# Half-wide diagonal blocks in the last batch and in the first two chunks, with reordered loads

## The chip, the cores and the metric

The kernel runs on one core of one Trainium2 chip. The metric is the device time of one execution in microseconds (us); smaller is better. Five engines work side by side, each on its own list of instructions in a fixed order, and they wait for one another through semaphores: TensorE (PE, matmul), whose weight loads the profile lists apart as PEld; VectorE (DVE); ScalarE (ACT); GpSimd (POOL), which does almost nothing here; and SyncE (SP), which issues the DMAs.

## The reference

Eight independent attentions without softmax, multiplied by `u`, feed a soft mixture of experts over all 19968 tokens.

```python
# u, v: (8, 2496, 256)   z: (8, 2496, 64)
scores = (1 / S) * np.matmul(z, z.transpose(0, 2, 1))
attn = np.maximum(scores, 0.0) ** 2
x = (u * np.matmul(attn, v)).reshape(B * S, D)
logits = x @ phi                                  # 32 slots, 4 for each of 8 experts
# softmax over all tokens -> slot_input = d.T @ x -> two-layer expert on each slot
# softmax over slots -> output = c @ slot_out
```

The scores of one batch form a symmetric matrix, because both factors are the same `z`. The kernel uses that: of a pair of blocks on the two sides of the diagonal it computes one, and gets the other by transposing it.

## The kernel before, in words

**Tiling.** The tokens of one batch are 20 tiles of 128 keys. Four tiles make a block `p` (0 to 4), and each batch has five query chunks `ch` of 512 columns (the fifth has 448; in the last batch the 448-wide chunk 4 stands first, and chunk 3 comes as two of 256). The unit of work is a *half*: two of a block's four key tiles (`w` is 0 or 1) against one chunk. A batch has 50 halves, the last one 60, the program 410; `h` counts them through, `at` is the place in the chunk. The tuple `MEETS` (`FIRST_MEETS` for batch 0) is the table that sets which blocks a chunk meets in which order. A plain number stands for both halves of a block, a pair such as `(2, 0)` for one half alone.

**One half.** `prepare(k)` (L311) makes the attention weights of half `k`: `scores(k)` on PE into the PSUM tile `sc`, Relu and Square on ACT into `r`, then a split of `r` into a rounded part `ph` and a remainder `pl`, so that three fast products (`ph` with both parts of `v`, `pl` with the high part) replace one slow one. `sums_halves` or `sums_whole` (L417, L451) multiply these with the split `v` into the accumulator `acc`. The first is used when a half ahead needs scores on PE; it runs as two phases with matmuls on 64 rows, paired on the two halves of the array, and `prepare` of the half two or three ahead goes between the phases. The second uses all 128 rows. For `k` under `RAW_SCORES` the scores come from unsplit `z` with slow fp32 matmuls, because the split `z` is not ready yet; otherwise from the split `z` in three products.

**Three kinds of half.** If the block on the other side of the diagonal has been done, the half is *turned*: its `r` is fetched from DRAM and no scores are computed. If its block will be wanted by a later chunk, DVE transposes `r` into a tile `y`, and `store` writes it out. A block on the diagonal is its own mirror: where it stands in the table as two pairs, the first half *lends* (DVE transposes 256 of its columns into `yd`, `lend` writes them to DRAM with four DMAs), and the second *borrows* (`borrow` reads them into `rd` with one DMA, its scores are only 256 columns wide, and ACT and DVE split the borrowed and the own part apart). Before the change that is done in batches 1 to 6 and in chunks 2 to 4 of batch 0.

**What sets the order.** Nothing is scheduled by a planner: every engine runs its instructions in the order in which the program writes them. The loop over `h` issues transfers (`transfers`, L767), the sums of half `h`, and the preparation of a half further on. Lists hold work that is run at fixed places in the next `prepare`: `turning` before the split of `r`, `behind` at its end (L368).

**Loads of the next batch.** In the loop from L757, `z_at` and `v_at` (L760) tell at which half, counted from the start of the batch before, the split of each block of `z` and of each of the ten tiles of `v` is due. The DMA is issued two halves earlier. The split (an ACT copy to the high part, a DVE subtraction for the low part) is appended to `behind` at that half and so stands at the end of the `prepare` that runs in it. Tile `i` of `v` holds the two key tiles of block `i // 2`, `w = i % 2`. The 16 buffers of `z` and `v` go round, 15 to a batch, so a tile takes over the buffer that the tile before it in the list had in the batch before.

**Opening of the program.** `opening` lists the loads of batch 0, `open_loads` issues them as the four raw buffers come free, and `keep_busy(n)` issues `n` pairs of filler matmuls on zeros into a tile `idle` that nobody reads.

Of the kernel before, what the change touches and what calls it, by code (L numbers as in the profile page):

```python
# [17 lines left out]
B, S, D, DQK = 8, 2496, 256, 64  # L18
N = B * S
E_, SE, FF = 8, 4, 1024  # L20
NS = E_ * SE
# [3 lines left out]
NQ = 5  # L25
# [4 lines left out]
NP = KT // 4  # L30
# [7 lines left out]
MEETS = (  # L38
# [3 lines left out]
)  # L42
FIRST_MEETS = ((0, 1, 2, 3, 4), (1, 0, 2, 4, 3)) + MEETS[0][2:]

FIRST_Z = {8: 1, 9: 2, 10: 4, 11: 3}

RAW_SCORES = 12

PAD = 224

# [1 line left out]
def f32(ap):  # L52
    return ap.bitcast(F32)
# [14 lines left out]
def attn_soft_moe_kernel(ctx, tc, uT, v, zz, phi, ww, outT):  # L68
    nc = tc.nc

    pe, act, dve, sp = (InOrder(tc, x) for x in (nc.tensor, nc.scalar, nc.vector, nc.sync))
# [48 lines left out]
    def load_v(b, i):  # L120
        raw = raws.tile([P, 2, D], F32, tag="raw", name=f"vr_{b}_{i}", bufs=NRAW)
        sp.dma_start(raw, v[b, :, 2 * i : 2 * i + 2, :])

        def split():
            t = vt_[b, i]
            (dve.tensor_copy if (b, i) == (0, 1) else act.copy)(t[:, :, 0], raw)
            dve.tensor_sub(t[:, :, 1], raw, f32(t[:, :, 0]))

        return split

    opening = []
    for p in range(NP):
        two = [(load_v, 2 * p), (load_v, 2 * p + 1)]
        opening += [(load_z, p)] + (two[::-1] if p == NQ - 1 else two)
    z_splits, v_splits = {}, []

    def open_loads(m):

        while opening and (len(v_splits) < m or opening[0][0] is load_z):
            f, j = opening.pop(0)
            if f is load_z:
                z_splits[j] = f(0, j)
            else:
                v_splits.append(f(0, j))


    ident = cpool.tile([P, P], F32, name="ident")
# [39 lines left out]
    def chunks(b):  # L189
        if b < B - 1:  # L190
            return [(j, 0, min(QC, S - j * QC), b * S + j * QC) for j in range(NQ)]
        t0 = b * S
        out = [(NQ - 1, 0, ROT, t0)]
        out += [(j, 0, QC, t0 + ROT + j * QC) for j in range(NQ - 2)]
        j = NQ - 2
        return out + [(j, o, QC // 2, t0 + ROT + j * QC + o) for o in (0, QC // 2)]
# [19 lines left out]
    halves = []  # L216
    for b in range(B):
        for ch, meets in zip(chunks(b), MEETS[b == B - 1] if b else FIRST_MEETS, strict=True):
            order = []
# [8 lines left out]

    pend, arriving, scratch, staged = {}, {}, {}, {}
    flag = cpool.tile([1, 1], F32, name="flag")
# [2 lines left out]
    middle, behind, stores, turning = [], [], [], []  # L236

    def run(todo):
        now, todo[:] = todo[:], []
        for f in now:  # L240
            f()
# [17 lines left out]
    def scores(k):  # L259
# [21 lines left out]

        if k < RAW_SCORES:
            for h, rows in enumerate(HALF):
# [16 lines left out]
    def high_low(k):  # L300

        if halves[k].ch[2] >= PAD + PAD:
            return [wa.tile([P, 2, QC], F32R, tag=t, name=f"{t}_{k}", bufs=4) for t in ("ph", "pl")]
        i, j = divmod(k % 4, 2)
        if i not in quarters:
            quarters[i] = [
                wa.tile([P, 2, 2, QC // 2], F32R, tag=t, name=f"{t}_{k}", bufs=4) for t in ("ph", "pl")
            ]
        return [t[:, j] for t in quarters[i]]

    def prepare(k):  # L311

        x = halves[k]
        n = x.ch[2]

        parts = [slice(0, 1), slice(1, 2)] if k < 2 else [slice(0, 2)]
        if x.turned:
            whole = arriving.pop(k)
            run(middle)
        else:  # L320
            r = wa.tile([P, 2, QC], F32, tag="r", name=f"r_{k}", bufs=4)
            ps, m = scores(k)
            for h in parts:
                act.activation(r[:, h, :m], ps[:, h, :m], AF.Relu, scale=1.0 / S)
                run(middle)
                act.activation(r[:, h, :m], r[:, h, :m], AF.Square)
            whole = r[:, :, :m].rearrange("p h (a r) -> p h a r", r=P // 2 if x.borrows else P)
        hi, lo = high_low(k)
        m = QC if x.padded else n
        hc, lc = (t[:, :, :m].rearrange("p h (a r) -> p h a r", r=P) for t in (hi, lo))  # L330
        cast = act.copy if x.turned or (x.turns and x.at % 3) else dve.tensor_copy
        run(turning)
        pieces = [(whole, slice(0, P), cast)]
        if x.borrows:
            lent = arriving.pop(k)
            pieces = [(lent, slice(0, P // 2), act.copy), (whole, slice(P // 2, P), dve.tensor_copy)]
        for h in parts:
            for src, cols, cast in pieces:
                cast(hc[:, h, :, cols], src[:, h])
                dve.tensor_sub(lc[:, h, :, cols], src[:, h], f32(hc[:, h, :, cols]))  # L340
        pend[k] = hi, lo
        if x.turns:
            key = x.b, x.ch[0], x.p
            first = key not in staged
            if first:
                staged[key] = turns_sb.tile([P, 16, 4, NS], F32, tag="y", name=f"y_{k}")
            y = staged[key]

            def turn():
                dve.transpose(  # L350
                    y.rearrange("p m i q -> p i m q")[:, 2 * x.w : 2 * x.w + 2],
                    r.rearrange("p h (m q) -> p h m q", q=NS),
                )
                if not first:
                    stores.append((k + (k < 2 * NP), lambda: store(key)))

            if k < 2 * NP:
                turning.append(turn)
            else:
                turn()  # L360
        if x.lends:
            y = turns_sb.tile([P, 4, 2, 2, NS], F32, tag="yd", name=f"yd_{k}", bufs=1)
            dve.transpose(
                y.rearrange("p a j i q -> p i a j q"),
                r.rearrange("p h (a i q) -> p h a i q", i=4, q=NS)[:, :, :, 2:4],
            )
            stores.append((k - 1, lambda: lend(x, y)))
        run(behind)  # L368

    def lend(x, y):  # L370

        key = x.b, x.p, x.p
        t = scratch[key] = dram.tile([P, 4, P], F32, tag="lent", name="lent_%d_%d" % key[:2], bufs=4)
        for a in range(4):
            sp.dma_start(
                t.rearrange("(b q) a r -> q b a r", b=4)[:, :, a],
                y[32 * a : 32 * a + 32].rearrange("q b j i k -> q b (j i k)"),
            )
# [8 lines left out]
    def store(key):  # L387

        y = staged.pop(key)
        t = scratch[key] = dram.tile([P, 4, QC], F32, tag="turned", name="turned_%d_%d_%d" % key)  # L390
        for a in range(4):
            sp.dma_start(
                t.rearrange("(b q) a r -> q b a r", b=4)[:, :, a],
                y[32 * a : 32 * a + 32].rearrange("q (b j) i k -> q b (j i k)", b=4),
            )
# [361 lines left out]
    for b in range(1, B):  # L757
        base, order = (b - 1) * 2 * NP * NQ, BLOCKS[b == B - 1]
        z_at = [29, 31, 33, 39, 41]
        v_at = [47, 42, 43, 44, 45, 46, 48, 49, 50, 51]  # L760
        for j, at in zip(order, z_at):
            splits.setdefault(base + at, []).append((load_z, b, j))
        for i, at in enumerate(v_at):
            splits.setdefault(base + at, []).append((load_v, b, i))
# [24 lines left out]
    def split_first_v():  # L789
        if v_splits:  # L790
            v_splits.pop(0)()
            open_loads(NRAW)
# [20 lines left out]
    def keep_busy(n):  # L813
        for _ in range(n):
            for h, rows in enumerate(HALF):
                pe.matmul(idle[:, h], zero[rows, 0:P], zero[rows], start=True, stop=True)

    take_blocks(0)
    open_loads(NRAW)
    keep_busy(7)  # L820
    split_first_v()
    split_first_v()
    prepare(0)
    prepare(1)
    keep_busy(5)
    constants()
    acc = None
    for h, x in enumerate(halves):
# [11 lines left out]
        if ahead and not halves[ahead[0]].turned:  # L840
            turn = sums_halves(h, acc, 0, None)
            prepare(ahead.pop(0))
            sums_halves(h, acc, 1, turn)
        else:
            if ahead and not x.ends:
                prepare(ahead.pop(0))
            elif not ahead:
                run(middle)
                run(behind)
                between_last(3 - last)  # L850
            sums_whole(h, acc)
# [12 lines left out]
    q = NQG - 1  # L864
    x = xg_.pop(q)
# [274 lines left out]
```

## Time and profile before

| what | value |
|---|---|
| median of 3 runs | 1359.9 us (1359.09 to 1360.61) |
| the profiled execution | 1361.58 us, its span 1359.8 us |
| PE busy | 1336.1 us, 98% of the span |
| DVE busy | 1084.2 us, 80% |
| ACT busy | 908.7 us, 67% |
| mean granted TensorE clock | 0.984 |

All attention work stands under one line of the code, since a helper records every instruction; rows are told apart by the names of the tiles: `sc`, `r`, `ph`, `pl`, `acc`, `y`, `yd`, `rd`, `v`, `vr` (raw `v`), `z`, `zr`, `cw` (which holds the raw `z` of batch 0), `xg` (a finished chunk), `lg` (logits and slot sums). In a timeline row the first number is the start in us from the start of the span, the second how long the merged instructions took, `xN` their count, and the brackets tell how long the engine was idle before and what ended that. A matmul on 64 rows comes in pairs that run together. The fillers and all other matmuls are told by the same two columns.

### The profile page before, as it was taken

How to read it: one execution, taken by the hardware profiler on the slowest of the kernel's cores; microseconds unless marked ns; L12 is line 12 of the kernel's file. 1: busy time of each engine (PE TensorE's matmuls, PEld its weight loads, DVE VectorE, ACT ScalarE, POOL GpSimd, SP SyncE). 2: the span in 40 equal slices, each digit the busy share in tenths (PEclk: the TensorE clock that was granted, in tenths of full speed). 3: DMA queues.
4: the chain of work that ended last, by engine and by line, in shares of the span. 5: the costliest groups of instructions: out<-in, count | busy, mean ns of one | idle time of the engine just before them, and what ended most of it. 6: DMA issues, size and time to landing. Idle time of an engine off the chain costs nothing.

```text
span 1359.8 us, 27351 instructions
## 1 busy us (share of the span) xinstructions
PE 1336.1 (98%) x10929; PEld 1062.3 (78%) x10929; DVE 1084.2 (80%) x1444; ACT 908.7 (67%) x1093; POOL 3.7 (0%) x22
## 2 busy tenths in 40 slices
PE   9999999999999999999999999999999999999985
PEld 6777887778777888778877788778877788778952
DVE  7878897779868898688987889797986889876563
ACT  8866686668755687566856678566875668654453
POOL 0000000000000000000000000000000000000000
PEclk9999999999999999999999999999999999999985
DMA  6568677675758667686776666777585776769969
GB/s 204 158 186 253 206 191 223 196 242 162 221 172 286 211 161 211 183 255 204 191 225 190 230 202 165 226 240 256 142 237 164 243 234 176 219 167 303 361 271 378
DMA packets 132511, 297.28 MB, mean 219 GB/s; under 512 B 17440, under 2 KB 36896, under 8 KB 120608
## 3 DMA queue, kind: packets, MB, share of 16 engines
q1 hardware_dynamic: 132384, 295.54, 70.6%
q8 instruction: 86, 1.41, 0.4%
q14 instruction: 41, 0.34, 0.1%
HBM read 161.25 MB, written 112.98 MB: 202 GB/s over the span
## 4 chain that ended last, share of the span: by engine, by line
PE 92%; ACT 2%; DMA 2%; DVE 2%; SPq 1%; issue 1%; DVEq 0%; ACTq 0%
PE acc L64 74%; PE sc L64 11%; PE lg L64 2%; PE pf L64 2%; SPq L64 1%; ACT r L64 1%; ACT ot L64 1%; PE po L64 1%; DMA lent<-yd 1%; PE h L64 1%; DMA outT<-ot 1%; DMA vr<-in_v 0%; ACT ph L64 0%; DVE pl L64 0%; PE idle L64 0%
## 5 line engine op out<-in xcount | busy, mean ns | idle before, releaser
L64 PE MATMUL acc<-ph,v 64*128 64x512 f32 (+5 forms) x5036 | 988.4, 387 | 0.0
L64 PEld LDWEIGHTS acc<-ph,v 64*128 64x128 f32 (+1 forms) x5036 | 593.5, 185 | 146.5 <-issue 24.9
L64 PE MATMUL acc<-pl,v 64*128 64x512 f32 (+5 forms) x2518 | 622.7, 383 | 1.5 <-DVE pl L64 1.5
L64 DVE TENSOR_TENSOR pl<-r,ph 128x1024 fp32r<-128x1024 f32 (+1 forms) x412 | 468.5, 1145 | 118.2 <-ACT ph L64 107.7
L64 ACT ACTIVATE r<-sc 128x1024 f32<-128x1024 f32 (+1 forms) x244 | 232.7, 954 | 194.6 <-PE sc L64 185.9
L64 ACT CAST ph<-r 128x1024 fp32r<-128x1024 f32 (+1 forms) x285 | 290.2, 1023 | 108.5 <-PE acc L64 77.1
L64 PEld LDWEIGHTS acc<-pl,v 64*128 64x128 f32 (+1 forms) x2518 | 306.8, 185 | 62.9 <-DVE pl L64 4.4
L64 ACT ACTIVATE r<-r 128x1024 f32<-128x1024 f32 (+1 forms) x244 | 241.1, 988 | 7.0
L64 DVE STREAM_TRANSPOSE y<-r 128x1024 f32<-128x1024 f32 x160 | 198.1, 1238 | 0.0
L64 PE MATMUL sc<-z,z 64*128 64x512 f32 x912 | 131.5, 393 | 0.2 <-ACT r L64 0.2
L64 DVE CAST ph<-r 128x1024 fp32r<-128x1024 f32 (+1 forms) x127 | 76.0, 598 | 40.9 <-ACT r L64 38.7
L64 PEld LDWEIGHTS sc<-z,z 64*128 64x128 f32 x912 | 85.0, 184 | 20.8 <-ACT r L64 0.6
L64 ACT CAST z<-zr 64x512 fp32r<-64x512 f32 x70 | 43.3, 619 | 56.2 <-DMA zr<-in_zz 55.0
L64 DVE TENSOR_TENSOR xg<-acc,ut 128x1024 f32<-128x1024 f32 (+7 forms) x57 | 48.4, 872 | 34.3 <-PE acc L64 34.3
L64 DVE TENSOR_TENSOR z<-zr,z 64x512 fp32r<-64x512 f32 x70 | 48.1, 687 | 21.5 <-ACT z L64 19.7
L64 DVE TENSOR_TENSOR v<-vr,v 128x512 fp32r<-128x512 f32 x80 | 53.6, 669 | 11.2 <-ACT v L64 11.1
L64 ACT CAST v<-vr 128x512 fp32r<-128x512 f32 x79 | 48.4, 613 | 17.9 <-DMA vr<-in_v 17.9
L64 PE MATMUL sc<-z 64*128 64x512 f32 (+1 forms) x468 | 54.7, 339 | 0.0
L64 DVE STREAM_TRANSPOSE y<-xg 128x512 f32<-128x512 f32 x72 | 49.5, 688 | 0.0
L64 PEld LDWEIGHTS sc<-z 64*128 64x128 f32 x468 | 41.1, 184 | 7.7
L64 DVE COPY ot<-pf 128x1024 f32<-128x1024 f32 (+2 forms) x22 | 24.3, 1103 | 21.9 <-PE pf L64 20.8
L64 ACT COPY ot<-pf 128x1024 f32<-128x1024 f32 (+2 forms) x22 | 20.1, 915 | 26.2 <-PE pf L64 24.7
(149 smaller groups left out, 481.0 us busy)
## 6 DMA issues: line engine op xcount, KB each, us to landing
turned<-y SPq DMA_DIRECT2D x320, 256.0 KB, 4.4
r<-turned SPq DMA_DIRECT2D x76, 1024.0 KB, 6.3
xt<-y SPq DMA_DIRECT2D x288, 72.0 KB, 3.4
vr<-in_v SPq DMA_DIRECT2D x80, 256.0 KB, 3.8
outT<-ot SPq DMA_DIRECT2D x16, 1024.0 KB, 6.9
ut<-in_uT SPq DMA_DIRECT2D x31, 512.0 KB, 5.3
zr<-in_zz SPq DMA_DIRECT2D x35, 256.0 KB, 5.5
lent<-yd SPq DMA_DIRECT2D x132, 64.0 KB, 2.5
```

The source lines that it names most:

```text
L64: return lambda *a, **k: self.tc.keep_in_program_order(f(*a, **k))
```

## The change

The table `MEETS` gets pairs for the diagonal blocks of the last batch's chunks 4, 0, 1 and 2, and `FIRST_MEETS` for chunks 0 and 1 of batch 0. In each of these six chunks the diagonal block's first half stands early in the chunk and its second half is now the last of the chunk (in chunk 2 of the last batch the sixth). With it the order of the other blocks in these chunks changes, the opening loads follow the order in which batch 0 meets its blocks (so `z` of block 1 and `v` tiles 2 and 3 come ahead of tile 1, which is now last), `v` tile 8 of the last batch is split one half earlier (at 49, where tile 7 was) and tile 7 one later, and the fillers go from 7 and 5 pairs to 5 and 4. The second `v` split of batch 0 is written between the first two preparations, with its high part on DVE. For half 0 the transposition into `yd` joins the list `turning`, which is now first run in the preparation of half 2.

```diff
 MEETS = (
     (((0, 0), 1, 2, 3, 4, (0, 1)), ((1, 0), 2, 4, 3, (1, 1), 0), (0, 1, (2, 0), 3, 4, (2, 1)),
      ((3, 0), 0, 1, 2, 4, (3, 1)), ((4, 0), 0, 1, 2, 3, (4, 1))),
-    ((0, 1, 2, 4, 3), (0, 4, 1, 2, 3), (0, 4, 1, 2, 3), (4, 2, 3, 0, 1), (0, 1, 2, 4, 3), (4, 3, 0, 1, 2)),
+    (((4, 0), 0, 1, 2, 3, (4, 1)), ((0, 0), 1, 4, 2, 3, (0, 1)), (0, (1, 0), 4, 2, 3, (1, 1)),
+     ((2, 0), 4, 3, (2, 1), 0, 1), (0, 1, 2, 4, 3), (4, 3, 0, 1, 2)),
 )
-FIRST_MEETS = ((0, 1, 2, 3, 4), (1, 0, 2, 4, 3)) + MEETS[0][2:]
+FIRST_MEETS = (MEETS[0][0], ((1, 0), 0, 2, 4, 3, (1, 1))) + MEETS[0][2:]
-RAW_SCORES = 12
+RAW_SCORES = 11
...
-            (dve.tensor_copy if (b, i) == (0, 1) else act.copy)(t[:, :, 0], raw)
+            (dve.tensor_copy if (b, i) == (0, 2) else act.copy)(t[:, :, 0], raw)
...
     opening = []
-    for p in range(NP):
-        two = [(load_v, 2 * p), (load_v, 2 * p + 1)]
-        opening += [(load_z, p)] + (two[::-1] if p == NQ - 1 else two)
+    for x in halves[: 2 * NP]:
+        if (load_z, x.p) not in opening:
+            opening.append((load_z, x.p))
+        opening.append((load_v, 2 * x.p + x.w))
...
-        run(turning)
+        if k > 1:
+            run(turning)
...
         if x.lends:
             y = turns_sb.tile([P, 4, 2, 2, NS], F32, tag="yd", name=f"yd_{k}", bufs=1)
-            dve.transpose(
-                y.rearrange("p a j i q -> p i a j q"),
-                r.rearrange("p h (a i q) -> p h a i q", i=4, q=NS)[:, :, :, 2:4],
-            )
-            stores.append((k - 1, lambda: lend(x, y)))
+            def turn():
+                dve.transpose(
+                    y.rearrange("p a j i q -> p i a j q"),
+                    r.rearrange("p h (a i q) -> p h a i q", i=4, q=NS)[:, :, :, 2:4],
+                )
+                stores.append((k - 1 + 2 * (k == 0), lambda: lend(x, y)))
+            if k:
+                turn()
+            else:
+                turning.append(turn)
...
-        v_at = [47, 42, 43, 44, 45, 46, 48, 49, 50, 51]
+        v_at = [47, 42, 43, 44, 45, 46, 48, *((49, 50) if b < B - 1 else (50, 49)), 51]
...
     open_loads(NRAW)
-    keep_busy(7)
-    split_first_v()
+    keep_busy(5)
     split_first_v()
     prepare(0)
+    split_first_v()
     prepare(1)
-    keep_busy(5)
+    keep_busy(4)
```

**Place 1, PE where the last batch begins (half 350).** In these lists the first number in a name is the half (`ph_350`), and for `v` the batch and the tile (`v_7_8` is tile 8 of the last batch, which counts as batch 7). Before:

```order
L64 MATMUL sc_352_13501<-z_7_4_12744,z_7_1_12746 128x512 x6
L64 MATMUL acc_17024_13205<-ph_349_13369,v_6_9_10854 128x448 x4
L64 MATMUL acc_17024_13205<-pl_349_13370,v_6_9_10854 128x448 x2
L64 MATMUL acc_17024_13205<-ph_349_13369,v_6_9_10854 128x448
L64 MATMUL acc_17024_13205<-pl_349_13370,v_6_9_10854 128x448
L64 MATMUL acc_17472_13531<-ph_350_13422,v_7_0_12749 128x448 x4
L64 MATMUL acc_17472_13531<-pl_350_13423,v_7_0_12749 128x448 x2
```

After:

```order
L65 MATMUL sc_352_13527<-z_7_4_12764,z_7_0_12765 128x512 x6
L65 MATMUL acc_17024_13225<-ph_349_13389,v_6_9_10874 128x448 x4
L65 MATMUL acc_17024_13225<-pl_349_13390,v_6_9_10874 128x448 x2
L65 MATMUL acc_17024_13225<-ph_349_13389,v_6_9_10874 128x448
L65 MATMUL acc_17024_13225<-pl_349_13390,v_6_9_10874 128x448
L65 MATMUL acc_17472_13556<-ph_350_13442,v_7_8_12777 128x448 x4
L65 MATMUL acc_17472_13556<-pl_350_13443,v_7_8_12777 128x448 x2
```

The first sums of the last batch read tile 8 of `v` where they read tile 0.

**Place 2, ACT and DVE at the same point.** ACT before:

```order
L64 CAST v_7_0_12749<-vr_7_0_13320 128x2x256
L64 ACTIVATE r_351_13457<-sc_351_13458 128x1024
L64 ACTIVATE r_351_13457<-r_351_13457 128x1024
L64 CAST ph_351_13467<-r_351_13457 128x1024
L64 CAST v_7_6_12755<-vr_7_6_13344 128x2x256
L64 ACTIVATE r_352_13500<-sc_352_13501 128x1024
L64 ACTIVATE r_352_13500<-r_352_13500 128x1024
L64 CAST ph_352_13510<-r_352_13500 128x1024
L64 CAST v_7_7_12756<-vr_7_7_13393 128x2x256
```

ACT after:

```order
L65 CAST v_7_0_12769<-vr_7_0_13340 128x2x256
L65 ACTIVATE r_351_13482<-sc_351_13483 128x1024
L65 ACTIVATE r_351_13482<-r_351_13482 128x1024
L65 CAST ph_351_13492<-r_351_13482 128x1024
L65 CAST v_7_6_12775<-vr_7_6_13364 128x2x256
L65 ACTIVATE r_352_13526<-sc_352_13527 128x1024
L65 ACTIVATE r_352_13526<-r_352_13526 128x1024
L65 CAST ph_352_13536<-r_352_13526 128x1024
L65 CAST v_7_8_12777<-vr_7_8_13413 128x2x256
```

DVE after (before, the third row is a transposition into `y` and the last reads `v_7_7`; the rest stands the same):

```order
L65 CAST ph_350_13442<-r_350_13432 128x1024
L65 TENSOR_TENSOR pl_350_13443<-r_350_13432,ph_350_13442 128x1024
L65 STREAM_TRANSPOSE yd_350_13446<-r_350_13432 128x2x8x32
L65 TENSOR_TENSOR v_7_0_12769<-vr_7_0_13340,v_7_0_12769 128x2x256
L65 TENSOR_TENSOR pl_351_13493<-r_351_13482,ph_351_13492 128x1024
L65 STREAM_TRANSPOSE y_351_13496<-r_351_13482 128x2x16x32
L65 TENSOR_TENSOR v_7_6_12775<-vr_7_6_13364,v_7_6_12775 128x2x256
L65 STREAM_TRANSPOSE cw_78<-L_15_12950 128x256
L65 TENSOR_TENSOR pl_352_13537<-r_352_13526,ph_352_13536 128x1024
L65 STREAM_TRANSPOSE y_351_13496<-r_352_13526 128x2x16x32
L65 TENSOR_TENSOR v_7_8_12777<-vr_7_8_13413,v_7_8_12777 128x2x256
```

Tile 8 stands in the slot that tile 7 had: on both engines behind the whole preparation of half 352.

**Place 3, ACT at the start of the program**, from the second Relu of half 1 on. Before:

```order
L64 ACTIVATE r_1_164<-sc_1_165 128x512
L64 ACTIVATE r_1_164<-r_1_164 128x512
L64 CAST v_0_2_108<-vr_0_2_122 128x2x256
L64 ACTIVATE r_2_225<-sc_2_226 128x1024
L64 ACTIVATE r_2_225<-r_2_225 128x1024
```

After:

```order
L65 ACTIVATE r_1_161<-sc_1_162 128x512
L65 ACTIVATE r_1_161<-r_1_161 128x512
L65 CAST ph_1_169<-r_1_161 128x512 x2
L65 CAST v_0_3_109<-vr_0_3_122 128x2x256
L65 ACTIVATE r_2_222<-sc_2_223 128x1024
```

Half 1 is now of block 1, whose split has its high part on ACT: two casts more stand ahead of the Relu of half 2.

More of the change, by code (lines that the diff above doesn't have):

```diff
@@ L125, in split @@
             t = vt_[b, i]
-            (dve.tensor_copy if (b, i) == (0, 1) else act.copy)(t[:, :, 0], raw)
+            (dve.tensor_copy if (b, i) == (0, 2) else act.copy)(t[:, :, 0], raw)
             dve.tensor_sub(t[:, :, 1], raw, f32(t[:, :, 0]))
         return split
-    opening = []
-    for p in range(NP):
-        two = [(load_v, 2 * p), (load_v, 2 * p + 1)]
-        opening += [(load_z, p)] + (two[::-1] if p == NQ - 1 else two)
[L137 to L146, printed above, removed]
     ident = cpool.tile([P, P], F32, name="ident")
@@ L225, in attn_soft_moe_kernel, with open_loads @@
             halves += [Half(b, ch, p, w, at, part) for at, (p, w, part) in enumerate(order)]
+    opening = []
+    for x in halves[: 2 * NP]:
+        if (load_z, x.p) not in opening:
+            opening.append((load_z, x.p))
+        opening.append((load_v, 2 * x.p + x.w))
+    z_splits, v_splits = {}, []
+    def open_loads(m):
+        while opening and (len(v_splits) < m or opening[0][0] is load_z):
+            f, j = opening.pop(0)
+            if f is load_z:
+                z_splits[j] = f(0, j)
+            else:
+                v_splits.append(f(0, j))
     pend, arriving, scratch, staged = {}, {}, {}, {}
@@ L362, in prepare @@
             y = turns_sb.tile([P, 4, 2, 2, NS], F32, tag="yd", name=f"yd_{k}", bufs=1)
-            dve.transpose(
-                y.rearrange("p a j i q -> p i a j q"),
-                r.rearrange("p h (a i q) -> p h a i q", i=4, q=NS)[:, :, :, 2:4],
-            )
-            stores.append((k - 1, lambda: lend(x, y)))
+            def turn():
[6 more added lines that the diff above has]
+                turn()
+            else:
+                turning.append(turn)
         run(behind)
```

## The prediction

> **What bounds the kernel now.** I read the page's busy shares and chain first, then the waits, then timelines around the places that the change touches.
>
> ```profile
> span 1359.8 us, 27351 instructions
> ...
> PE 1336.1 (98%) x10929; PEld 1062.3 (78%) x10929; DVE 1084.2 (80%) x1444; ACT 908.7 (67%) x1093; POOL 3.7 (0%) x22
> ...
> PE 92%; ACT 2%; DMA 2%; DVE 2%; SPq 1%; issue 1%; DVEq 0%; ACTq 0%
> ```
>
> PE is busy for 98% of the span and holds 92% of the chain that ended last. A busy PE can still be stretched, so the chain of waits in order of time shows the beat; the first number is the start.
>
> ```profile
> 11.12 2.81 PE acc L64 x24
> 14.79 2.80 PE acc L64 x24
> ...
> 57.35 2.79 PE acc L64 x24
> 60.84 2.79 PE acc L64 x24
> ```
>
> A half in batch 0's chunk 0 comes 3.67 us after the one before (14.79 - 11.12), one in chunk 1 3.49 us after (60.84 - 57.35). Of that 2.80 us are sums and the rest scores: 0.87 us raw, 0.70 us from split `z`. The sums run without a gap. The list of waits says the same from the other side:
>
> ```profile
> ACT r L64 <- PE sc L64: 185.9, 142, 4.3
> ```
>
> ACT waits for PE's scores 142 times; PE waits for others almost nowhere. So the kernel is a sum of PE work, and two things move the time: matmul columns taken off PE, and any place where PE must wait anew.
>
> **The change part by part.** The price of a half-wide score, from PE's timeline in batch 0's chunk 2, where it exists already:
>
> ```profile
> 100.93 0.52 PE L64 MATMUL sc<-z 64*128 64x256 f32 x6
> 101.29 0.64 PE L64 MATMUL acc<-ph,v 64*128 64x512 f32 x4
> ...
> 103.87 0.86 PE L64 MATMUL sc<-z 64*128 64x512 f32 x6
> 104.57 0.63 PE L64 MATMUL acc<-ph,v 64*128 64x512 f32 x4
> ...
> 105.28 0.39 PE L64 MATMUL acc<-pl,v 64*128 64x512 f32 x1
> 105.60 0.73 PE L64 MATMUL acc<-ph,v 128*128 128x512 f32 x2
> 106.17 0.39 PE L64 MATMUL acc<-pl,v 128*128 128x512 f32 x1
> ```
>
> Start to start it takes 0.36 us against 0.70, so one block saves 0.34. *Last batch:* four blocks, **-1.4**. *Batch 0:* chunk 1 loses two raw scores (1.74) and gets one raw and one half-wide (0.87 + 0.36), -0.5. Chunk 0 has its last raw score at half width; no row shows one, so its saving lies between 0 and 0.87. I take half, since the split score falls almost in proportion: -0.4. Together **-0.9**.
>
> The last three rows show the change from 64 to 128 rows: 0.89 us for three steps that take 0.23 each elsewhere (2.80 for twelve pairs), about 0.2 lost. The last batch's new order makes half 369 prepare scores between halves that don't, so it has nine such changes in place of seven; one coincides with a return from the logits, which costs the same already. **+0.2**.
>
> A borrowed block adds five DMA issues, a 0.70 us transposition and one more split piece; DVE and ACT have 20% and 33% of the span free, and `yd` and `rd` are asked for five or more halves ahead, as in batches 1 to 6. Nothing on PE's path.
>
> *Start of the program.* Chain of waits first, then two timelines:
>
> ```profile
> 1.19 3.17 PE idle L64 x14
> ...
> 6.98 1.08 PE idle L64 x10
> ```
> ```profile
> 3.73 0.76 PEld L64 LDWEIGHTS sc<-cw 64*128 64x128 f32 x4 [0.28 <-DMA cw<-in_zz]
> 4.15 2.83 PE L64 MATMUL sc<-cw 64*128 64x512 f32 x8
> ...
> 5.83 0.43 DVE L64 CAST v<-vr 128x512 fp32r<-128x512 f32 x1 [0.32 <-DMA vr<-in_v]
> ...
> 11.23 1.02 ACT L64 ACTIVATE r<-sc 128x1024 f32<-128x1024 f32 x1
> ...
> 14.46 1.23 DVE L64 TENSOR_TENSOR pl<-r,ph 128x1024 fp32r<-128x1024 f32 x1 [1.85 <-ACT ph L64]
> ```
>
> `z` of block 0 is there at 3.73, but the fillers hold PE until 4.15; five pairs at 0.45 (3.17 for 7) end at 3.4, so the first scores come 0.4 earlier. Half 1 is now of block 1, whose `z` takes the third DMA's place, that of `v` tile 1, which DVE saw at 5.83: PE stands idle for about 0.4 between the two scores, under ACT's work on half 0. But two casts of 0.6 (place 3) now stand ahead of half 2's Relu: 11.23 - 0.4 + 1.2 = 12.0. Its `pl`, at 14.46 before, runs from about 15.3 to 16.5, and PE reaches it at about 16.2. PE waits 0.3, and I allow 0.1 for half 3. **0.0** in all, between -0.4 (all hidden) and +0.7.
>
> *Chunks 0 to 1 of batch 0.* PE waited here before:
>
> ```profile
> 51.95 0.51 PE L64 MATMUL acc<-pl,v 64*128 64x512 f32 x2 [0.45 <-DVE pl L64]
> ```
>
> DVE's queue of `pl`, `z` splits and the finished chunk is late there. In the new order the first turned half comes one half earlier, with the same DVE work and `yd` (0.7) ahead of it, while an order by which a half with its high part on DVE follows the short half 15 takes away a smaller wait. **0.0**, between -1.0 and +0.6.
>
> *Tile 8 of `v` in the last batch.* This decides. Place 1 of the order: the first sums of half 350 read tile 8. Place 2: its split stands in tile 7's old slot. The timeline of ACT, DVE and PE at that slot:
>
> ```profile
> 1117.30 0.60 ACT L64 CAST v<-vr 128x512 fp32r<-128x512 f32 x1
> ...
> 1120.45 0.86 PE L64 MATMUL sc<-z,z 64*128 64x512 f32 x6
> ...
> 1120.90 0.65 DVE L64 TENSOR_TENSOR v<-vr,v 128x512 fp32r<-128x512 f32 x1
> ...
> 1121.96 0.57 PE L64 MATMUL acc<-ph,v 64*128 64x448 f32 x4
> 1122.04 1.02 ACT L64 ACTIVATE r<-sc 128x1024 f32<-128x1024 f32 x1
> ...
> 1124.18 1.05 ACT L64 CAST ph<-r 128x1024 fp32r<-128x1024 f32 x1
> ...
> 1125.13 0.62 ACT L64 CAST v<-vr 128x512 fp32r<-128x512 f32 x1
> 1125.27 1.23 DVE L64 TENSOR_TENSOR pl<-r,ph 128x1024 fp32r<-128x1024 f32 x1 [0.31 <-ACT ph L64]
> ...
> 1126.41 1.24 DVE L64 STREAM_TRANSPOSE y<-r 128x1024 f32<-128x1024 f32 x1
> 1127.57 0.65 DVE L64 TENSOR_TENSOR v<-vr,v 128x512 fp32r<-128x512 f32 x1
> ```
>
> The first and third rows are tile 0's two splits, which the old first sums need: done at 1121.55, just ahead of PE's first pair at 1121.96. The tile now needed first has its high part at 1125.75 and its low part at 1128.22. That can't come sooner: ACT must first work off half 352, whose scores PE issues at 1120.45, and on DVE the low part stands behind that half's `pl` and `y`. The saved 0.54 of `yd` against `y` ends in DVE's 0.31 wait for `ph`. PE does its first pair at 1125.8, then waits again; the second pair, due at 1122.2, starts at 1128.3. Behind it in PE's order stand the scores of half 353, so nothing fills the gap. **+6.0**, between 5.4 (ACT and DVE without any backlog) and 6.3.
>
> Some of it comes back. In the old order ACT was late one half further on:
>
> ```profile
> 1122.98 0.36 PE L64 MATMUL acc<-pl,v 64*128 64x448 f32 x2
> 1123.19 0.89 PE L64 MATMUL sc<-z,z 64*128 64x512 f32 x6
> ...
> 1126.16 0.36 PE L64 MATMUL acc<-pl,v 64*128 64x448 f32 x2
> 1126.73 0.97 PE L64 MATMUL sc<-z,z 64*128 64x512 f32 x6 [0.21 <-ACT r L64]
> ```
>
> Scores follow the last pair by 0.21 in one half and by 0.57 in the next, and the logits behind them wait for the finished chunk too. After a pause of 6 us ACT and DVE have caught up. **-0.6**, between -0.8 and 0.
>
> *The clock.* What an idle PE costs afterwards is to be seen only at the end of the span, by stretches (busy PE, its share, granted clock before the DMA columns):
>
> ```profile
> 1303.13:1306.54 3.41, 2.33 (x41) 1.40 (x43) 1.86 (x4) 1.44 (x3) 0.00 (x0) 1.00 0.13 54
> 1306.54:1309.95 3.41, 3.41 (x30) 1.91 (x30) 1.23 (x1) 1.01 (x1) 0.00 (x0) 0.50 0.63 253
> 1309.95:1313.37 3.42, 3.42 (x62) 2.14 (x62) 2.38 (x2) 2.02 (x2) 0.00 (x0) 1.00 1.02 422
> ```
>
> After 3.41 us with 2.33 busy the next 3.41 run at half clock, and only a full stretch brings it back. The new gap leaves about 0.4 of 6 us busy. Where the stretches' edges fall is open, so PE comes back at half clock for some 3.4 to 6.4 us. What half clock costs, the fillers show: 14 matmuls in 3.17 us at the start (0.45 a pair), 10 in 1.08 (0.22) six us later. For sums I take the same 0.45 against their 0.23, a loss of 0.49 of the time: 1.7 to 3.1, **+2.3** from near the middle; 0 if the clock stays.
>
> [...]
>
> **Sum:** -1.4 - 0.9 + 0.2 + 0.0 + 0.0 + 6.0 - 0.6 + 2.3 = **+5.6 us**. The profiled execution took 1361.58 (1.8 around its span), 1.7 over the median of the runs; it would become 1367.2. Set against the median of 1359.9: **1365.5 us**.
>
> **The rivals.** (1) *The clock stays up.* For it: one pair falls into the gap, and DVE's rows may come somewhat earlier; against it, the row at 1303.13. Sum without 2.3: +3.3, 1363.2. (2) *The tile is in time,* and the change is only its saved columns. It decides from the point where both parts of tile 8 are done by 1122.2, six us before the old slot. For it: tile 0's slot, two halves earlier, does make it. Against it: the order puts the split behind half 352 on both engines. Sum -1.4 - 0.9 + 0.2 = -2.1, less perhaps 0.4 at the start: 1357.6, not slower. [...]
>
> **How the numbers follow.** Forecast 0.68, rival 1 0.16, rival 2 0.07, rival 3 0.09. The forecast's own terms give 1363.5 to 1367.2; rival 1 and rival 3 widen that to **1361.8 to 1367.6**, with half of rival 1's lower tail and rival 2 left out. A change under 0.2% (2.7 us) can't be told from none: slower means over 1362.6. The forecast lies above it almost wholly, rival 1 by about two thirds, rival 3 wholly: slower 0.86; rival 2 and the rest are mostly within 0.2%: same 0.11, faster 0.03.
>
> **What would show it.** In the changed profile: PE idle before `acc<-ph` near 1121 for 3.7 us, put down to ACT `v`, and again for 2.2 to DVE `v`; half clock in the stretch after; the scores of the half after that without a wait for ACT. 64x256 scores 0.36 long in batch 0 and the last batch. At the start the first `sc` at 3.7. It is wrong if PE shows no gap there, or if the gap is under 3 us.

## The result, and the profile after

The changed kernel took **1365.65 us** (median) against 1359.83 of the kernel before in the same session: a ratio of **1.0048, 95% interval 1.0036 to 1.0059**, 5.8 us slower. The prediction said 1365.5. Among the runs below there is one slow one in experiment 1 (2177.86 us) and one in experiment 6 (2630.96 us), which the ratios leave out.

In the profiled execution of the changed kernel (1367.4 us) the page's first lines and the chain by engine read:

```profile
span 1365.5 us, 27408 instructions
...
PE 1334.7 (98%) x10925; PEld 1061.8 (78%) x10925; DVE 1084.9 (79%) x1452; ACT 909.3 (67%) x1103; POOL 3.7 (0%) x22
...
PE 92%; DMA 3%; ACT 2%; DVE 2%; issue 1%; SPq 0%; DVEq 0%; ACTq 0%
```

PE's busy time fell by 1.4 us (1336.1 to 1334.7) and the span grew by 5.7, so the time in which PE stands grew by 7.1 (23.7 to 30.8). In PE's list of waits (us in total, times, longest) the sums and scores of the kernel before had these two lines:

```profile
PE acc L64 <- DVE pl L64: 1.5, 2, 1.1
...
PE sc L64 <- ACT r L64: 0.2, 1, 0.2
```

The list of the changed kernel has three that were not there before:

```profile
PE acc L65 <- ACT v L65: 3.7, 1, 3.7
PE acc L65 <- DVE v L65: 1.9, 1, 1.9
...
PE sc L65 <- DMA cw<-in_zz: 0.8, 1, 0.8
```

The third is at the start of the program, where half 1 waits for `z` of block 1. The first two, 5.6 us together, are one place, the start of half 350, the last batch's first. ACT, DVE and PE there, from the timeline of the changed kernel; what stands in brackets is the engine's idle time ahead of the row and what ended it:

```profile
1121.61 0.36 PE L65 MATMUL acc<-pl,v 64*128 64x448 f32 x1
...
1122.94 1.06 ACT L65 ACTIVATE r<-r 128x1024 f32<-128x1024 f32 x1
...
1124.03 1.04 ACT L65 CAST ph<-r 128x1024 fp32r<-128x1024 f32 x1
...
1124.98 0.61 ACT L65 CAST v<-vr 128x512 fp32r<-128x512 f32 x1
1125.11 1.23 DVE L65 TENSOR_TENSOR pl<-r,ph 128x1024 fp32r<-128x1024 f32 x1 [0.29 <-ACT ph L65]
1125.64 0.53 PE L65 MATMUL acc<-ph,v 64*128 64x448 f32 x2 [3.67 <-ACT v L65]
1126.25 1.24 DVE L65 STREAM_TRANSPOSE y<-r 128x1024 f32<-128x1024 f32 x1
1127.41 0.65 DVE L65 TENSOR_TENSOR v<-vr,v 128x512 fp32r<-128x512 f32 x1
...
1128.11 0.74 PE L65 MATMUL acc<-ph,v 64*128 64x448 f32 x2 [1.94 <-DVE v L65]
...
1130.14 1.48 PE L65 MATMUL sc<-z,z 64*128 64x512 f32 x6
...
1131.67 1.02 ACT L65 ACTIVATE r<-sc 128x1024 f32<-128x1024 f32 x1 [6.08 <-PE sc L65]
```

The high part of tile 8 comes behind the whole of half 352 on ACT, its low part behind that half's `pl` and `y` on DVE. PE gets one pair done at 1125.64 and the second at 1128.11. Afterwards the sums and scores take longer than elsewhere (0.95 for four sums, 1.48 for six scores, against 0.57 and 0.86). The same time in stretches of 3.41 us, laid on the steps at which the granted clock changes in this trace (PE's busy time first, then the other engines'; the granted clock is the number ahead of the DMA columns, 1.00 in the second row):

```profile
1119.10:1122.51 3.41, 2.88 (x28) 2.23 (x24) 2.58 (x4) 3.35 (x5) 0.00 (x0) 1.00 0.49 132
1122.51:1125.93 3.42, 0.28 (x2) 0.19 (x2) 3.13 (x5) 3.02 (x4) 0.00 (x0) 1.00 0.38 98
1125.93:1129.34 3.41, 1.47 (x8) 1.15 (x8) 3.19 (x5) 0.00 (x0) 0.00 (x0) 0.50 0.30 65
1129.34:1132.75 3.41, 3.41 (x20) 2.88 (x20) 0.00 (x0) 1.05 (x2) 0.00 (x0) 0.50 0.97 230
1132.75:1136.17 3.42, 3.42 (x34) 3.08 (x34) 2.32 (x3) 2.33 (x3) 0.00 (x0) 1.00 0.93 264
```

After a stretch with 0.28 us of PE work two stretches ran at half clock.

Cut into stages, in us of the profiled executions. A half ends with its last sums on PE; the logits that PE does behind half 351 are counted with that half. "Again" is a second profile of the changed kernel and "by use" the kernel of the first experiment, both from below:

| stage | before | changed | changed, again | by use |
|---|---|---|---|---|
| start to the end of half 2 | 19.85 | 20.98 | 19.83 | 19.42 |
| halves 3 to 19 (rest of chunk 0, chunk 1) | 58.13 | 57.58 | 57.56 | 57.54 |
| halves 20 to 349 (code unchanged) | 1044.14 | 1043.42 | 1042.56 | 1042.13 |
| half 350 | 3.18 | 11.44 | 11.18 | 3.18 |
| half 351 and the logits behind it | 5.79 | 5.03 | 5.03 | 5.79 |
| halves 352 to 389 | 120.54 | 119.50 | 119.50 | 119.45 |
| the rest | 108.2 | 107.6 | 107.7 | 107.5 |
| span | 1359.8 | 1365.5 | 1363.3 | 1355.0 |

Half 350 alone lost 8.26 us (11.44 - 3.18); all other rows together gained 2.6. Not all of that is the change's: the two rows of 20 to 349 and of the rest hold code that is unchanged but for load times, and over the nine profiles of this document they range from 1042.1 to 1045.4 and from 107.5 to 108.2.

### The profile page after: what moved, and what is told of

The parts are those of the page before. It is cut to its first block, busy times and chain, and to the rows that moved or that the text cites. A ratio compares the mean times of both kernels' runs of the same rounds, so it can differ in the third digit from the quotient of the medians.

```text
span 1365.5 us, 27408 instructions
## 1 busy us (share of the span) xinstructions
PE 1334.7 (98%) x10925; PEld 1061.8 (78%) x10925; DVE 1084.9 (79%) x1452; ACT 909.3 (67%) x1103; POOL 3.7 (0%) x22
## 4 chain that ended last, share of the span: by engine, by line
PE 92%; DMA 3%; ACT 2%; DVE 2%; issue 1%; SPq 0%; DVEq 0%; ACTq 0%
PE acc L65 75%; PE sc L65 11%; PE lg L65 2%; PE pf L65 1%; DMA outT<-ot 1%; ACT r L65 1%; PE po L65 1%; DMA xt<-y 1%; ACT ot L65 1%; PE h L65 1%; DMA zr<-in_zz 0%; DVE pl L65 0%; SPq L65 0%; ACT ph L65 0%; DMA vr<-in_v 0%
## 5 line engine op out<-in xcount | busy, mean ns | idle before, releaser
L65 ACT CAST ph<-r 128x1024 fp32r<-128x1024 f32 (+1 forms) x289 | 293.3, 1020 | 107.6 <-PE acc L65 78.7
L65 DVE CAST ph<-r 128x1024 fp32r<-128x1024 f32 (+1 forms) x123 | 72.3, 588 | 45.8 <-ACT r L65 42.3
L65 PE MATMUL sc<-z 64*128 64x256 f32 (+1 forms) x474 | 53.9, 332 | 0.0
```

The lines of the kernel that those rows point to most:

```text
L65: return lambda *a, **k: self.tc.keep_in_program_order(f(*a, **k))
```

## The experiments

**1. Is the late tile all that is wrong in the last batch?** The order of meeting stays as changed; only the places of the `v` tiles, and with them their buffers and split times, follow the order of use, so that tile 8 gets the first slot, tile 0's before.

```diff
+LAST_V = 8, 0, 1, 2, 3, 4, 5, 6, 7, 9
-        for i in range(2 * NP):
+        for i in range(2 * NP) if b < B - 1 else LAST_V:
             vt_[b, i] = blk.tile(...)
...
-        v_at = [47, ..., 48, *((49, 50) if b < B - 1 else (50, 49)), 51]
+        v_at = [47, ..., 48, 49, 50, 51]
...
-        for i, at in enumerate(v_at):
+        for i, at in zip(range(2 * NP) if b < B - 1 else LAST_V, v_at):
```

> The changed kernel, with the last batch's tiles of v given their places in the order in which its first chunk uses them (8, 0, 1, ... 7, 9), so that tile 8 takes the first place, which tile 0 had before. Theory (tile 8 is late, and nothing else in the last batch is): PE's two waits at half 350 (3.67 and 1.94 us) and the stretch at half clock after them go, and the 0.76 us that came back at half 351 goes too: 6.0 + 2.3 - 0.8 = 7.5 us less than the changed kernel, about 1358.1 us. Rival A (the wait moves on: another tile of v is now the late one): a PE wait of over 1 us within halves 351 to 357, 1359.5 to 1363 us. Rival B (the borrowed blocks themselves cost in the last batch): no wait, but at least 1362 us.

Measured: 1357.63 us, 0.9986 of the kernel before (0.9977 to 0.9995). ACT and PE at half 350 in its timeline:

```profile
1118.48 0.62 ACT L66 CAST v<-vr 128x512 fp32r<-128x512 f32 x1
...
1118.73 0.36 PE L66 MATMUL acc<-ph,v 64*128 64x448 f32 x1
1118.73 0.36 PE L66 MATMUL acc<-pl,v 64*128 64x448 f32 x1
1118.93 0.57 PE L66 MATMUL acc<-ph,v 64*128 64x448 f32 x4
...
1123.70 0.97 PE L66 MATMUL sc<-z,z 64*128 64x512 f32 x6 [0.21 <-ACT r L66]
```

The first sums of half 350 (1118.93) follow the last of half 349 without a gap, half 350 takes 3.18 us again, and the small wait for ACT at the following half's scores is back, as in the kernel before. No other tile became late, and halves 352 to 389 keep their gain: both rivals fall. Some eight microseconds hang on the order in which the tiles take their places. This version is faster than both kernels, by 0.14% against the kernel before.

**2. What is the change worth without the last batch?** The last batch's table and split times are those of before; batch 0 and the start stay changed.

```diff
-    (((4, 0), 0, 1, 2, 3, (4, 1)), ((0, 0), 1, 4, 2, 3, (0, 1)), ...),
+    ((0, 1, 2, 4, 3), (0, 4, 1, 2, 3), ...),
-        v_at = [47, ..., 48, *((49, 50) if b < B - 1 else (50, 49)), 51]
+        v_at = [47, ..., 48, 49, 50, 51]
```

> The changed kernel with the last batch's table and its split times as before, so that only batch 0 and the start are changed. Theory from the two traces (the start lost 1.1 us, half 8 lost 0.4, the half-wide scores gained 0.9): +0.6 us over the kernel before, 1360.4 us, no wait near half 350. Rival, the prediction's own terms (scores -0.9, start and chunks 0 to 1 at nothing): 1358.9 us.

Measured: 1358.79 us, 0.9997 (0.9989 to 1.0006), 0.5 us under the 1359.34 of before in that session. The reading of the two traces, by which the start was dearer by 1.1 us, gave the wrong sign; the prediction's own terms (0.9 less) are nearer. But the interval (1.5 us less to 0.8 more) holds both expectations and nothing at all, so that the medians don't decide; experiment 5 does. Against experiment 1 it is 1.2 us slower (1358.79 - 1357.63), which is what the last batch's half-wide blocks bring when no tile is late: the prediction had -1.4 + 0.2 for them, and the stage of halves 352 to 389 says 1.1.

**3. Is the loss after the gap the clock?** Tile 8 stays late, but PE is given useless matmuls in both gaps.

```diff
...
+            if k == 350 and phase == 0 and i < 2:
+                gap_fill((28, 14)[i])    # pairs of 64x256 bf16 matmuls into a spare bank
             for h, rows in enumerate(HALF):
                 vp, pp = todo[h][i]
```

> The changed kernel with idle matmuls (64x256 bf16, from the identity into a spare bank) in PE's two gaps at half 350: 28 pairs before its first sums, 14 pairs before its second. Tile 8 is as late as in the changed kernel. Theory (the slow stretch after the gap is the clock, lowered because PE was idle): the granted clock stays 1.00 from 1110 to 1140 us, the first real sums of half 350 start as late as before (near 1125.6 and 1128.1), and the 2.3 us after them are saved: 1363.3 us. Rival (the sums after the gap are slow for another reason, or the clock follows useful work alone): 1365.6 us, and half clock from 1126 to 1133 as in the changed kernel.

Measured: 1362.56 us, 1.0024 (1.0014 to 1.0034). PE's timeline and the stretches on the clock's steps of this kernel:

```profile
1119.43 3.23 PE L65 MATMUL gap<-ident 64*128 64x256 bf16 x56
1123.25 0.47 PE L65 MATMUL acc<-ph,v 64*128 64x448 f32 x2 [0.59 <-ACT v L65]
1123.56 1.70 PE L65 MATMUL gap<-ident 64*128 64x256 bf16 x28
1125.72 0.47 PE L65 MATMUL acc<-ph,v 64*128 64x448 f32 x2 [0.45 <-DVE v L65]
...
1126.84 0.86 PE L65 MATMUL sc<-z,z 64*128 64x512 f32 x6
```
```profile
1122.06:1125.48 3.42, 2.61 (x42) 1.76 (x36) 3.12 (x4) 1.14 (x2) 0.00 (x0) 1.00 0.02 5
1125.48:1128.89 3.41, 3.17 (x30) 2.85 (x32) 1.25 (x3) 1.11 (x2) 0.00 (x0) 1.00 0.81 190
```

Half 349 had ended at 1119.43 but for the fillers; the second real pair comes 6.29 us later (1125.72), against 6.29 in the changed kernel (1128.11 - 1121.82, the time 0.21 after its last sum's start). The wait is the same, the clock stays at 1.00, the next scores take 0.86 in place of 1.48, and from the end of half 348 to the end of half 350 it takes 11.88 us against 13.97 and 13.71 in the two profiles of the changed kernel. So half clock cost 1.8 to 2.1 us; the rival falls, and here the clock stayed up with idle matmuls in the gap (2.61 of 3.42 us busy in the stretch from 1122.06, where the changed kernel had 0.28 in its stretch from 1122.51). Of the medians the ratios differ by 0.0024, 3.3 us, more than the trace accounts for but within what their intervals leave open; against the second measurement of the changed kernel (1.0040, experiment 5) it is 2.2 us.

**4. Is the start dearer for want of fillers?** The changed kernel with as many as before.

```diff
-    keep_busy(5)
+    keep_busy(7)
...
-    keep_busy(4)
+    keep_busy(5)
```

> The changed kernel with the start's fillers as many as before (7 pairs and 5 pairs in place of 5 and 4). Theory (the start is dearer because PE's holes put off the first rise of the clock from 6.06 to 9.77 us): the clock rises at 6 to 7 us, half 0 ends about 1 us earlier (12.6 in place of 13.66), 1364.6 us. Rival (the z of block 1 lands late, and fillers only move the first scores back): the clock rises at 9 to 10 us again and half 0 ends at 13.7 or later, 1365.6 to 1366 us.

Measured: 1365.23 us, 1.0044 (1.0032 to 1.0056); no difference from the changed kernel that could be told. In its profile the clock rose at 4.91 us, which looks like the theory; but the three kernels above have the changed kernel's 5 and 4 pairs, and theirs rose at 4.86, 7.19 and 5.90. The question was wrong: not the number of fillers but the single execution set what I had read as the start's price. That is the next experiment.

**5. The changed kernel once more.** No edit.

> The changed kernel itself once more. Four kernels with the same first half so far raised the clock at 9.77, 4.86, 7.19 and 5.90 us and ended half 0 at 13.66, 11.72, 12.22 and 12.14. Theory (the moment of the first rise varies from execution to execution, and the changed kernel's 1.1 us at the start were chance): the rise comes anywhere from 4.8 to 9.8 us, half 0 ends between 11.7 and 13.7, both gaps at half 350 and the half clock after them stand as before, median 1365 to 1365.9 us. Rival (the start of the changed kernel is really dearer): rise at 9.8 and half 0 at 13.7 again.

Measured: 1365.57 us, 1.0040 (1.0028 to 1.0053). The clock rose at 7.16 us, half 0 ended at 12.12 (13.66 in the first profile, 12.52 in the kernel before), and the end of half 2, at 19.83, is that of the kernel before. The 1.1 us at the start were no fixed cost; they went with the moment of the first rise. The late tile is there again, with waits of 3.7 and 1.7 us in half 350.

**6. What does chunk 0's half-wide block bring?** As experiment 1, but chunk 0, the opening loads and the fillers as before; chunk 1 keeps its half-wide block. The diff shows the table alone; the edit also puts back the places of the first two `v` splits and the 7 and 5 pairs.

```diff
-FIRST_MEETS = (MEETS[0][0], ((1, 0), 0, 2, 4, 3, (1, 1))) + MEETS[0][2:]
+FIRST_MEETS = ((0, 1, 2, 3, 4), ((1, 0), 0, 2, 4, 3, (1, 1))) + MEETS[0][2:]
...
```

> As the kernel in which tile 8 is in time (places of v by use), but chunk 0 of batch 0 meets its blocks as before, with the loads, the splits and the 7 and 5 pairs of fillers of before; chunk 1 keeps its half-wide block. The prediction's terms: chunk 0's half-wide raw score (0.43 us less) is given up, and nothing else: 0.4 us more, 1358.0 us. Theory from the traces: with it goes the wait of 0.4 us at half 8 that came with the short half 7, so the time is the same, 1357.6 us, and from the end of half 0 to the end of half 19 the trace shows 65.2 us in both. Rival (chunk 0's borrowed block also loads DVE ahead of chunk 1 and causes the wait of 0.74 us for DVE pl at half 11): that wait goes too, 64.5 us there and 1356.9 us in all.

Measured: 1358.68 us, 0.9989 (0.9980 to 0.9998); by the ratios 0.4 us more than experiment 1 (0.0003 of 1360), which the intervals can't separate from nothing. Its trace takes 65.77 us from the end of half 0 to that of half 19, experiment 1's 65.24 and the first profile of the kernel before 65.46. DVE's queue ahead of half 11 in this kernel, and PE's waits in halves 10 and 11:

```profile
43.58 1.23 DVE L66 TENSOR_TENSOR pl<-r,ph 128x1024 fp32r<-128x1024 f32 x1 [0.51 <-DVE ph L66]
44.73 0.70 DVE L66 STREAM_TRANSPOSE yd<-r 128x512 f32<-128x512 f32 x1
45.46 1.41 DVE L66 TENSOR_TENSOR z<-cw,z 64x512 fp32r<-64x512 f32 x2
46.79 1.21 DVE L66 TENSOR_TENSOR xg<-acc,ut 128x1024 f32<-128x1024 f32 x1
47.93 1.21 DVE L66 TENSOR_TENSOR pl<-r,ph 128x1024 fp32r<-128x1024 f32 x1
```
```profile
44.86 0.50 PE L66 MATMUL acc<-pl,v 128*128 128x512 f32 x1 [0.29 <-DVE pl L66]
...
49.19 0.51 PE L66 MATMUL acc<-pl,v 64*128 64x512 f32 x2 [1.07 <-DVE pl L66]
```

DVE works without a pause from 43.58 to 49.14, and PE waits for the last of it. The `yd` in this row is chunk 1's own, so taking chunk 0's block away doesn't take the wait away: it grew from 0.74 to 1.07, and the rival falls. The theory by which the two versions come out the same in the trace falls in its sum (65.77 against 65.24), but not in its step: halves 7 and 8 together take 6.62 us in both, so there the raw columns saved and the wait behind the short half do cancel. What it missed comes after them: the halves 10 and 11 take 0.55 and 0.33 us more in this kernel, both behind waits for DVE `pl`, and half 2, with the opening of before, takes 0.37 less. So the prediction's +0.4 agrees with the medians in its size, but its reason, the 0.43 of the raw score alone, is not what the trace shows.

**7. The same late slot, used later.** The changed kernel with one chunk in another order.

```diff
-    (((4, 0), 0, 1, 2, 3, (4, 1)), ((0, 0), 1, 4, 2, 3, (0, 1)), ...
+    ((0, 1, (4, 0), 2, 3, (4, 1)), ((0, 0), 1, 4, 2, 3, (0, 1)), ...
```

> The changed kernel, with the last batch's first chunk in the order 0, 1, (4, 0), 2, 3, (4, 1): tile 8 keeps the late slot that the change gave it, but is first used in half 354 in place of half 350; tile 0, in its old slot, is used first. Theory (the late slot costs only because the first sums need the tile): no wait of PE at 350 or 354, full clock throughout, 1357.6 us as with the places by use. Rival (a half-wide pair in the middle of the chunk, lent later and borrowed five halves on, makes PE wait for the borrowed block, or the slot is late for half 354 too): a PE wait of over 1 us between halves 353 and 359, 1359 us or more.

Measured: 1358.45 us, 0.9987 (0.9978 to 0.9996). Halves 350 to 359 show one PE wait, the old one (0.20 us):

```profile
1128.42 0.97 PE L65 MATMUL sc<-z 64*128 64x512 f32 x6 [0.20 <-ACT r L65]
```

Tile 8 is split in the changed kernel's slot, and nothing waits for it, since half 354 is the first to need it. So two edits of different kinds, one of the slot and one of the order, each take the loss away. Its profiled execution took 1362.2 us, 3.7 over the median. What it has more than that of experiment 1 lies mostly in the unchanged halves 20 to 349 (1045.37 us against 1042.13), with the wait in the row below in batch 4, which comes after a load of `z` for which ACT had waited 7.95 us (until 757.52), and at the start, where the clock rose only at 10.17 us (half 2 ends at 20.88 against 19.42); halves 352 to 389 took 119.50 us, as in experiment 1.

```profile
765.20 0.97 PE L65 MATMUL sc<-z,z 64*128 64x512 f32 x6 [1.54 <-ACT r L65]
```

## Why the prediction was right, and where its terms were off

**The bound.** PE's work, its clock and its waits set the time: by the page PE was busy 1.4 us less, although part of its work ran at half clock, and stood 7.1 us more, 5.6 of it in the two waits at half 350. The experiments that took these two waits away took the loss away.

**Tile 8, +6.0.** Right, by its mechanism and its size. Predicted were the first pair at 1125.8 and the second at 1128.3, six late; the rows have 1125.64 and 1128.11, against 1122.02 if there had been no wait (0.20 after a first pair at 1121.82), so 6.1. The releasers are those named, ACT `v` and then DVE `v`. Experiment 1 makes the tile in time and experiment 7 lets nothing need it early; in both, half 350 and half 351 with its logits are back at 3.2 and 5.8 us, 7.5 less in all.

**The clock, +2.3.** Right in its size: half 350's remaining loss is 8.26 - 6.1 = 2.2, and experiment 3 measures 1.8 to 2.1 apart from the wait. One detail differs: the clock fell not when PE came back for good but at 1125.93, before the second wait, so that 1.9 us of the 6.8 at half clock (the stretch from 1125.93 has 1.47 of 3.41 us busy) fell on an idle PE and cost nothing. The row on which the term rested, half clock after a stretch with 2.33 of 3.41 us busy, is no rule. In experiment 4's kernel, the same gap stands otherwise to the clock's steps:

```profile
1117.65:1121.07 3.42, 1.82 (x18) 1.25 (x14) 2.83 (x4) 3.36 (x5) 0.00 (x0) 1.00 0.46 101
1121.07:1124.48 3.41, 0.47 (x2) 0.19 (x2) 3.12 (x5) 1.98 (x3) 0.00 (x0) 1.00 0.21 71
1124.48:1127.90 3.42, 2.30 (x12) 2.08 (x14) 2.13 (x4) 0.00 (x0) 0.00 (x0) 0.50 0.60 131
```

After a stretch with 1.82 of 3.42 us busy the clock was still up; after the next, with 0.47, it was at half. In the second profile of the changed kernel it fell after one with 0.04. So the share of busy time alone does not decide, and what does stays open. That the term came out is luck in part: in all three profiles that have this gap unfilled the clock fell, after 0.28, 0.47 and 0.04 us of work, but that does not follow from the row at 2.33. The way back is as the prediction read it: in the changed kernel's profile a stretch at half clock with 1.47 us busy was followed by another, the one with 3.41 by full clock.

**What comes back, -0.6.** Right: half 351 and the logits behind it gave back 0.76 (5.79 to 5.03) in both profiles. Of that 0.47 lies in the half (3.61 to 3.14), whose scores started without waiting for ACT, and 0.29 in the logits, both as foreseen; experiment 1 got the wait of 0.21 back with the rest.

**Last batch's scores, -1.4 + 0.2.** Halves 352 to 389 took 1.0 us less in both profiles of the changed kernel and 1.1 less in experiment 1; the medians of experiments 1 and 2 differ by 1.2. The half-wide score keeps its price there, 0.35 from start to start in the changed kernel's timeline:

```profile
1152.30 0.52 PE L65 MATMUL sc<-z 64*128 64x256 f32 x6
1152.65 0.59 PE L65 MATMUL acc<-ph,v 64*128 64x448 f32 x4
```

**Batch 0's scores, -0.9, and chunks 0 to 1, 0.0.** The first is right, the second is where the prediction was off. The columns are saved: the raw half-wide score, for which no row existed, takes 0.43 (half of 0.87) as the prediction took it: half 7 took 2.53 us, where the short half of the kernel before took 2.96. But halves 3 to 19 gained 0.55, not 0.9. The term set at 0.0 was mis-sized; it was about +0.4. Two waits in the changed kernel show where:

```profile
36.64 0.59 PE L65 MATMUL sc<-cw 64*128 64x256 f32 x4
...
38.80 0.50 PE L65 MATMUL acc<-pl,v 64*128 64x512 f32 x2 [0.16 <-DVE pl L65]
...
49.47 0.50 PE L65 MATMUL acc<-pl,v 64*128 64x512 f32 x2 [0.76 <-DVE pl L65]
```

The first is a new wait for DVE `pl` at half 8, behind the short half 7: 4.08 us in place of the 3.66 of any full half with raw scores, which takes back the 0.43 that half 7 gained. The second is the backlog of DVE, longer than the 0.45 of before, since chunk 1's `yd` and the turned half's `pl` now stand ahead of it. Against these two, smaller losses of the kernel before are gone, as the prediction expected of one: half 11 took 3.06 us there where its sums need 2.80, and half 17 took 3.65 where halves of its kind take 3.49. While DVE is the late one there, part of what is taken off PE's columns comes back as waiting.

**The start, 0.0.** Right as a typical value and meaningless for one execution: in six profiles with this opening half 2 ended at 20.98, 19.42, 19.71, 19.86, 19.83 and 20.88, four of them within 0.5 of the 19.85 of before and two a microsecond above it; the mean is 20.11. The small wait foreseen for half 2 was there when the clock rose early (at 4.86 to 7.19 us, where half 2 took 4.04, 3.82, 4.05 and 4.06 us) and hidden when it rose late (at 9.77 and 10.17, where it took 3.66). The range's upper end has in it 0.6 us for a late first rise of the clock, which was the author's estimate and which no run shows: in the two profiles with the late rise half 2 ended 1.1 and 1.0 us after the 19.85 of before, and in the second profile of the changed kernel, with the rise at 7.16, no later than before (19.83).

**The sum.** By the table the terms come to 6.1 + 2.2 - 0.8 - 1.0 - 0.5 = +6.0 with the start at nothing, beside the predicted +5.6 and the measured +5.8 and +5.7 (1365.57 - 1359.88) of the medians. Errors of up to 0.4 in single terms went in both directions, so that the sum came within 0.2 us of the first median is luck in part. The sum without the late tile, -2.1 to -2.5 in rival 2, was -1.7 in experiment 1 (1357.63 - 1359.34): the same 0.4 that batch 0 fell short. That the terms were set against the median and not the profiled span was needed: the first profile of the kernel before spent 2.0 us more in the unchanged halves 20 to 349 than that of experiment 1 (1044.14 against 1042.13).

## What to carry to other kernels

When an order of work is changed, list what the first instruction of each stage now reads and in which slot that is made; a list of slots that is "about the same" can hold the one tile that everything waits for, and then the fix is to give out slots in order of use. The gap on PE had two prices here, the wait (6.1 us) and the slow time after it (2.2), and they can be measured apart by filling the gap with idle work. What a single profile shows at the start of a program has to be seen in a second one before it is called a cost.

## What the runs showed of the hardware beyond what was expected

The first rise of PE's clock came at a different time in each profile. Six profiles with the same opening have it at 9.77, 4.86, 7.19, 5.90, 7.16 and 10.17 us, and half 0 ends between 11.72 and 13.66 us with it. The first rows of the kernel of experiment 1 and of the changed kernel:

```profile
3.47 1.80 PE L66 MATMUL sc<-cw 64*128 64x512 f32 x4
5.86 1.13 PE L66 MATMUL sc<-cw 64*128 64x512 f32 x4 [0.59 <-DMA cw<-in_zz]
...
7.49 0.82 PE L66 MATMUL acc<-ph,v 64*128 64x512 f32 x4
```
```profile
3.49 2.08 PE L65 MATMUL sc<-cw 64*128 64x512 f32 x4
...
6.34 2.08 PE L65 MATMUL sc<-cw 64*128 64x512 f32 x4 [0.78 <-DMA cw<-in_zz]
...
9.56 0.91 PE L65 MATMUL acc<-ph,v 64*128 64x512 f32 x4
```

With the clock up at 4.86 the first raw scores at full clock bring the first sums at 7.49, with it up at 9.77 they start at 9.56. The two profiles with the opening of before, that of the kernel before and that of experiment 6, have the rise at 6.06 and 7.18 and half 0's end at 12.52 and 12.51; whether that opening is steadier, two executions can't say. Unchanged code moves a single execution by more: halves 20 to 349 took 3.2 us longer in the profile of experiment 7, the one with the late load of `z`, than in that of experiment 1.
